# A linear-attention and ELU feed-forward kernel: u of the first four spans in quarters of the array, y's last quarter by DMA from span 2 on, a smaller v, and a new order of the opening

## The chip, the cores and the metric

The kernel runs on one core of one Trainium2 chip. The metric is the device time of one launch in microseconds; 0.2% of it, about what a measurement of this kernel can tell from no change, is 1.0 us.

## The reference, cut to what matters

```python
# q, k, v, alpha: 4 batches x 8 heads x 768 steps x 48
for t in range(S):
    state = alpha[:, :, t, :, None] * state + einsum('bhd,bhe->bhde', k[:, :, t], v[:, :, t])
    y[:, :, t] = einsum('bhd,bhde->bhe', q[:, :, t], state)
x = y.transpose(0, 2, 1, 3).reshape(3072, 384)
h = x @ w_in                                     # 384 -> 2048
g = where(h > 0, h, exp(min(h, 0)) - 1)
out = g @ w_out                                  # 2048 -> 384
```

All inputs and the output are float32.

## The kernel before, in words

**Spans.** A batch's 768 steps are cut into 6 spans of 128 steps, so there are 24 spans, 0 to 23; two neighbouring spans make a block of 256 tokens, 0 to 11. Within a span the recurrence is done by matmuls on two chunks of 64 steps (index c or x), for 4 pairs of heads (n, two heads a = 0, 1 to a pair). For span i the code has small functions, called tokens, that are named by two or three letters: `L`, `LA`, `LB` load q, k and alpha; `LV` loads v; `SC` forms the running product of alpha (`P`) by a scan on DVE; `LN`, `EX` its inverse on ACT; `KA`, `KB`, `KC`, `SQ` scale k and q (DVE or POOL, by the tables `KAV` to `SQV`); `TP`, `KN` (spans 0 to 5, on PE and ACT) or `TA`, `TB` (later, on DVE) transpose k; `S` is the score matmul and `MK` its mask; `U` (L380) is the product of transposed k and v for either chunk; `UA`, `UB`, `UC` (L421 to L443) turn u into the states that the second chunk and the next span start from; `Y` (L489) multiplies scores by v and q by the state. `XH`, `XP`, `XL` split y into an upper and a lower part, fp32r each, in the tile `xt` of the block.

**The form of u.** For spans from `QU` = 6 on, `U` hands over to `U4` (L367), which gives every matmul one quarter of the array (64 rows by 64 columns), so that four of them run side by side; u of chunk 1 is then only that chunk's own sum, and `UB` subtracts it from the state that `UA` has made. For spans 0 to 5 `U` makes two passes by halves: chunk 1 sums over all 128 steps, in 128 rows by 64 columns, and chunk 0 over 64. In span 1 (`UPE`) the old state is added to u on PE, by two matmuls with a matrix `minus` (`UP`, L414), and `UA` is a copy on ACT.

**y's last quarter.** y has 4 pairs of 96 features, but `xt` holds 3 rows of 128: each of these takes one pair's 2 x 48 features and 2 x 16 features of the last pair. For spans below `DIRECT` = 4 the last pair is made first (`YL`), copied to SBUF by ACT (`Y3`), and spread into the three by six matmuls with a selecting matrix `sel` (L497) ahead of the other three pairs. For later spans all four pairs are made at once, ACT and DVE split the last pair into `y3` like the rest, and `XD` (L541) moves it into `xt` by two DMAs of the SP queue.

**Feed-forward.** Block b goes through 8 steps j of 256 hidden features: `A.b.j` (18 matmuls, L655) makes h; `RA`, `RB` (ACT), `RC` (DVE) make the ELU; `GH` (ACT) and `GL` (DVE, L692) split it; `O.b.j` (12 matmuls, L706) adds to the output, which `Z` copies and stores. Weights arrive as raw 64-bit words (`F.f`, 768 KB each, 16 of them); DVE decodes a pair of them (`DA`, `DB`, `DC`, 128x1536 each, 8 pairs), `WH` (ACT) rounds to the upper part, `WL` forms the lower part (POOL, for some DVE, or PE and ACT by `WP`).

**What sets the order.** No scheduler does. The string `START` lists the tokens of the opening (spans 0 to 11, blocks 0 to 3 in part, all the weights), the string `STEADY` a period that is repeated after it. Each token records its instructions when it is called, so the lists fix what stands in which place on every engine's in-order queue and on the SP queue that issues the DMAs. PSUM tiles come from a pool of eight banks.

Of the kernel before, what the change touches and what calls it, by code (L numbers as in the profile page):

```python
# [49 lines left out]
U.1 XH.0 F.6 DC.0 UP.1 LN.2 XP.0 EX.2 KA.2 SQ.2 MK.1 UA.1 F.5 WH.0 WP.0 YL.1 F.1 F.3 UC.1 Y3.1 KB.2 SC.3 KC.2  # L50
WH.2 XL.0 PC.2 LN.3 DA.2 EX.3 SQ.3 Y.1 DB.2 KA.3 XH.1 TP.2 WP.2 DC.2 KB.3 KN.2 DA.1 DB.1 XP.1 KC.3 U.2 XL.1
WL.2 LC.0 WL.0 S.2 A.0.0 RA.0.0 WH.6 WL.6 F.7 A.0.1 MK.2 UB.2 UA.2 TP.3 LV.3 UC.2 S.3 L.4 KN.3 F.9 YL.2 U.3
WH.4 SC.4 WL.4 Y3.2 Y.2 UA.3 PC.3 RB.0.0 MK.3 XH.2 DA.3 SQ.4 DC.1 DB.3 YL.3 LN.4 XL.2 Y3.3 UB.3 A.0.2 LV.4
WH.3 EX.4 F.10 CA.0 F.8 WL.3 Y.3 A.0.3 XH.3 UC.3 DC.3 XL.3 L.5 F.12 RA.0.1 KA.4 KB.4 A.1.1 A.1.0 LV.5 F.11
# [34 lines left out]
def gla_elu_ffn(ctx: ExitStack, tc: tile.TileContext, qka, vv, vn, wgt, out):  # L89
# [174 lines left out]
    @tok  # L264
    def ZS(i):
        if EARLY <= i < QS:
            for a in range(2):
                nc.gpsimd.memset(win[i]["st"][64 - 64 * a:128 - 64 * a, a], 0.0)


    @tok
# [95 lines left out]
    def U4(i):  # L367
        d = win[i]
        q4, begun = shared(i)
        d["u"] = [t[:, 0:NP * D].rearrange("p (n e) -> p n e", n=NP) for t in q4]  # L370
        for n in range(NP):
            for x, a in QUADS if i % NW < NW - 1 else QUADS[::2]:
                r = slice(64 * x, 64 * x + 64)
                nc.tensor.matmul(d["u"][x][64 * a:64 * a + 64, n, :], lhsT=d["kn"][r, n, a, :],  # L374
                                 rhs=d["vn"][r, 2 * n + a, :], start=(n == 0 and x not in begun), stop=True,
                                 skip_group_check=True)
        begun.update((0, 1) if i % NW < NW - 1 else (0,))

    @tok
    def U(i):  # L380
# [4 lines left out]
        d["u"] = [u[:, 0], u[:, 1]]
        m = 64 if i < EARLY else D
        for x in ((1, 0) if i % NW < NW - 1 else (0,)):
            r = slice(0, C) if x == 0 and i < EARLY else slice(0, 128)
            v = d["vn"] if x or i < EARLY else v0[i % 2].rearrange("p (h e) -> p h e", e=D)
            for n in range(NP):  # L390
                for a in range(2):
                    nc.tensor.matmul(d["u"][x][64 * a:64 * a + m, n, :], lhsT=d["kn"][r, n, a, 0:m],  # L392
                                     rhs=v[r, 2 * n + a, :],
                                     start=(x == int(i % NW < NW - 1) and n == 0), stop=True, skip_group_check=True)
# [9 lines left out]

    def diff(i, out, r, x):
        u = win[i]["u"][x][r]
        half = i >= QU and x == 1
        if (i % NW == 0 or i in UPE) and not half:
            nc.scalar.mul(out=out, in_=u, mul=-1.0)  # L409
        else:  # L410
            nc.vector.tensor_tensor(out=out, in0=state(i, r, int(half)), in1=u, op=ALU.subtract)  # L411
# [556 lines left out]
```

## Time and profile before

| | |
|---|---|
| median of 3 runs | 504.48 us (504.24 to 504.65) |
| span of the profiled execution, first to last instruction | 502.5 us |
| time outside that span (median less span) | 2.0 us |
| TensorE clock granted, mean | 0.999 |
| HBM read, written | 53.53 MB, 4.72 MB |

The profile is of one execution. PE is the matmul engine's row, PEld its weight loads, which run beside the matmuls; DVE, ACT and POOL are the vector, scalar and general engines; SPq is the queue of SP that issues nearly all DMAs. A row of a timeline gives the start and the length in us, then engine, line, operation, output tile and inputs. A float32 matmul stands as two records; an fp32r one as one.

### The profile page before, as it was taken

The numbers are of one execution on the slowest core, as the hardware profiler recorded it, in microseconds if no ns is written. First come the engines' busy times: TensorE is split into PE (matmuls) and PEld (weight loads), VectorE is DVE, ScalarE is ACT, GpSimd is POOL, SyncE is SP. The second block draws the span as 40 slices with busy tenths as digits, with TensorE's granted clock in tenths as the row PEclk, the third lists the DMA queues.
The fourth block names the chain that finished last, engine by engine and source line by source line (L and its number), as shares of the span: only waits on it lengthen the run. The fifth ranks groups of instructions, "written<-read, shape, count | busy, mean of one in ns | idle before, by whom it ended". The sixth has DMA issues, their size and how long they took to land.

```text
span 502.5 us, 13254 instructions
## 1 busy us (share of the span) xinstructions
PE 492.4 (98%) x5404; PEld 476.0 (95%) x5404; DVE 386.6 (77%) x807; ACT 289.5 (58%) x689; POOL 129.4 (26%) x111
## 2 busy tenths in 40 slices
...
DMA  8999324222521145226135145234332321110001
GB/s 311 412 411 382 91 95 165 64 59 100 190 59 64 57 130 178 65 83 219 54 119 178 48 119 182 63 112 172 82 112 97 95 76 44 56 42 8 3 33 36
DMA packets 22403, 61.13 MB, mean 122 GB/s; under 512 B 2880, under 2 KB 9792, under 8 KB 22336
## 3 DMA queue, kind: packets, MB, share of 16 engines
...
HBM read 53.53 MB, written 4.72 MB: 116 GB/s over the span
## 4 chain that ended last, share of the span: by engine, by line
PE 96%; DVE 2%; ACT 1%; issue 1%; ACTq 0%
PE o L706 40%; PE h L655 40%; PE y L458 4%; PE y L453 2%; PE q L374 2%; PE q L330 2%; PE u L392 1%; PE sc L346 1%; PE wp L126 1%; PE y L497 1%; PE tp L282 1%; DVE kn L292 0%; PE yl L453 0%; PE wd L628 0%; DVE st L358 0%
## 5 line engine op out<-in xcount | busy, mean ns | idle before, releaser
L655 PE MATMUL h<-xt,w 128*128 128x256 f32 x1728 | 215.0, 282 | 0.0
L655 PEld LDWEIGHTS h<-xt,w 128*128 128x128 f32 x1728 | 209.3, 188 | 1.8
L706 PE MATMUL o<-w,gh 128*128 128x384 f32 x768 | 199.3, 341 | 0.6 <-ACT gh L679 0.6
L706 PEld LDWEIGHTS o<-w,gh 128*128 128x128 f32 x768 | 136.9, 188 | 1.6 <-ACT gh L679 0.8
L706 PE MATMUL o<-w,gl 128*128 128x384 f32 x384 | 130.0, 339 | 0.1
L679 ACT CAST gh<-h 128x512 fp32r<-128x512 f32 x96 | 55.9, 583 | 79.6 <-DVE h L673 39.3
L692 DVE TENSOR_TENSOR gl<-h,gh 128x512 fp32r<-128x512 f32 x96 | 65.5, 687 | 35.5 <-ACT gh L679 34.2
L292 DVE STREAM_TRANSPOSE kn<-qka 32x128 f32<-32x128 f32 x288 | 87.0, 302 | 4.5
L663 ACT ACTIVATE r<-h 128x512 f32<-128x512 f32 x96 | 57.0, 595 | 47.2 <-PE h L655 40.7
L673 DVE SCALAR_TENSOR_TENSOR h<-r,h 128x512 f32<-128x512 f32 x96 | 64.6, 689 | 16.9 <-ACT r L668 16.1
L706 PEld LDWEIGHTS o<-w,gl 128*128 128x128 f32 x384 | 72.1, 188 | 0.4 <-DVE gl L692 0.4
L231 POOL TENSOR_TENSOR qka<-qka,R 128x512 f32<-128x512 f32 x19 | 26.1, 1375 | 164.6 <-DVE gl L692 127.6
L668 ACT ACTIVATE r<-r 128x512 f32<-128x512 f32 x96 | 59.4, 631 | 0.7
L261 POOL TENSOR_TENSOR st<-qka,P 64x512 f32<-64x512 f32 x36 | 42.8, 1189 | 21.7 <-DVE P L209 16.2
L358 DVE TENSOR_TENSOR st<-q,mask 64x256 f32<-64x256 f32 x72 | 30.4, 422 | 12.0 <-ACT vs L409 9.2
L209 DVE TENSOR_TENSOR_SCAN P<-qka,first 128x516 f32<-128x516 f32 x24 | 30.6, 1275 | 1.6 <-DMA qka<-in_qka_dram 1.2
L236 POOL TENSOR_TENSOR R<-P,R 128x512 f32<-128x512 f32 x20 | 24.2, 1211 | 27.3 <-DVE qka L231 25.9
L218 ACT ACTIVATE R<-P 128x512 f32<-128x512 f32 x24 | 15.2, 632 | 27.8 <-DVE P L209 27.8
L411 DVE TENSOR_TENSOR vs<-vs,q 48x192 f32<-48x192 f32 x30 | 10.5, 350 | 19.1 <-PE q L330 16.9
L511 ACT ACTIVATE y<-y 128x128 fp32r<-128x128 f32 x20 | 5.5, 275 | 30.0 <-PE y L458 26.6
L639 POOL TENSOR_TENSOR w<-spare,w 128x768 fp32r<-128x768 f32 x7 | 15.8, 2256 | 26.0 <-ACT w L619 13.9
L611 ACT ACTIVATE ck<-ck,lim 128x384 f32<-128x384 f32 x32 | 20.6, 644 | 0.1
...
## 6 DMA issues: line engine op xcount, KB each, us to landing
...
raw<-in_wgt_dram SPq DMA_DIRECT2D x16, 768.0 KB, 12.3
...
xt<-y SPq DMA_DIRECT2D x40, 48.0 KB, 2.3
...
```

The source lines that it names most:

```text
L209: nc.vector.tensor_tensor_scan(out=P.rearrange("p n w -> p (n w)"), data0=t[:, 2 * NP * W:], data1=first.rearrange("p n w -> p (n w)"), in ...
L231: eng(KAV, i).tensor_tensor(out=d["kt"], in0=d["kt"], in1=d["R"], op=ALU.mult)
L261: eng(SQV, i).tensor_tensor(out=st[r, a], in0=d["q"][r], in1=pw(i)[r], op=ALU.mult)
L292: nc.vector.transpose(out=kn[32 * t:32 * t + 32, :, 32 * g:32 * g + 32], in_=d["kt"][32 * g:32 * g + 32, :, 32 * t:32 * t + 32])
L358: nc.vector.tensor_tensor(out=d["st"][r, a, :, c * C:(c + 1) * C], in0=d["s4"][a][o], in1=mask[o].unsqueeze(1).broadcast_to([64, NP, C]), ...
L655: nc.tensor.matmul(h[:, f, :], lhsT=t[:, wi, ws], rhs=x[:, c, xi, :], start=(f == 0 and k == 0), stop=(k == 8), skip_group_check=True)
L663: nc.scalar.activation(out=r, in_=d["h"], func=AF.Relu, scale=-1.0)
L668: nc.scalar.activation(out=d["r"], in_=d["r"], func=AF.Exp, scale=-1.0)
L673: nc.vector.scalar_tensor_tensor(out=d["h"], in0=d["r"], scalar=-1.0, in1=d["h"], op0=ALU.add, op1=ALU.max)
L679: nc.scalar.copy(out=gh, in_=d["h"])
L692: nc.vector.tensor_tensor(out=gl, in0=d["h"], in1=d["gh"].bitcast(F32), op=ALU.subtract)
L706: nc.tensor.matmul(o[:, 0:DM], lhsT=gt[:, f, ms], rhs=t[:, wi, f * DM:f * DM + DM], start=(j == 0 and f == 0 and k == 0), stop=(j == NJ - ...
```

## The change

Five things are changed at once.

1. `QU` = 6 becomes the set `UQ`: spans 0 to 3 too take `U4`. With it `UPE` is empty: the two matmuls of `UP` in span 1 go; `UA` of span 1 moves from ACT to DVE; `UB` of spans 0 and 1 is now a DVE subtraction (it did not exist there).
2. `DIRECT` = 4 becomes 2: spans 2 and 3 lose `YL`, `Y3` and the `sel` matmuls, make four pairs in one `Y`, and take `XH`, `XL` with `y3` and the two DMAs of `XD`. For spans 0 and 1, y and yl now share a PSUM tile.
3. v of spans from 6 on is loaded without its doubled quarter: two DMAs of 64 x 576 instead of 64 x 768 words each. `U4` finds v in the first or the last part of the tile by the new `vrow`.
4. In `U4` the weights of spans from 6 on are 48 columns wide, not 64, as only 48 of the rows of u are read.
5. `START` is a new list of the same steps; two zeroed tiles `v0` that nothing used go, and the two unused steps `V0` and `ZS`.

```diff
-DIRECT = 4
+DIRECT = 2
-QU, QS = 6, 6
+UQ, QS = (0, 1, 2, 3, *range(EARLY, NWIN),), EARLY
-WPE, XPE, GPE, UPE = (0, 2), (0, 1), (), (1,)
+WPE, XPE, GPE, UPE = (0, 2), (0, 1), (), ()
 START = """
-LA.0 LB.0 SC.0 LN.0 EX.0 LA.1 KA.0 KB.0 LB.1 SC.1 X.2 LV.0 LN.1 X.2 KC.0 F.2 SQ.0 EX.1 F.0 TP.0 KN.0 S.0 U.0
+LA.0 SC.0 LA.1 LN.0 X.2 LB.0 EX.0 SC.1 LB.1 LN.1 F.0 SQ.0 KA.0 KB.0 KC.0 S.0 F.2 EX.1 KA.1 SQ.1 KB.1 MK.0 TP.0 LV.0
...
-            nc.sync.dma_start(out=vs[0:64, 0:2 * HD], in_=vv[i, 0:64])
-            nc.sync.dma_start(out=vs[64:128, HD:3 * HD], in_=vv[i, 64:128])
+            nc.sync.dma_start(out=vs[0:64, 0:HD + HH], in_=vv[i, 0:64, 0:HD + HH])
+            nc.sync.dma_start(out=vs[64:128, 2 * HD - HH:3 * HD], in_=vv[i, 64:128, 0:HD + HH])
+    def vrow(i, x, a, n):
+        r = slice(64 * x, 64 * x + 64)
+        if i < EARLY:
+            return win[i]["vn"][r, 2 * n + a, :]
+        if a == x:
+            o = HD + n * D + x * HH
+            return vs_t[i % NB][r, o:o + D]
+        return lhs(i, x, a)[r, n * D:(n + 1) * D]
...
     def U4(i):
+        m = 64 if i < EARLY else D
-                nc.tensor.matmul(d["u"][x][64 * a:64 * a + 64, n, :], lhsT=d["kn"][r, n, a, :],
-                                 rhs=d["vn"][r, 2 * n + a, :], start=(n == 0 and x not in begun), stop=True,
+                nc.tensor.matmul(d["u"][x][64 * a:64 * a + m, n, :], lhsT=d["kn"][r, n, a, 0:m],
+                                 rhs=vrow(i, x, a, n), start=(n == 0 and x not in begun), stop=True,
                                  skip_group_check=True)
...
     def diff(i, out, r, x):
-        half = i >= QU and x == 1
+        half = i in UQ and x == 1
...
     def UB(i):
-        if i % NW < NW - 1 and (i >= QU or i % NW and i not in UPE):
+        if i % NW < NW - 1 and (i in UQ or i % NW and i not in UPE):
...
     def YL(i):
-        yl = d["yl"] = psa.tile([128, W], F32, name="yl", tag="pa")
+        d["y"] = psa.tile([128, NP, W], F32, name="y", tag="pa")
+        yl = d["yl"] = d["y"][:, NP - 1]
```

What the new list moves is seen in the order of the queues. First the SP queue, whose rows are the first DMAs of the kernel (128x516 is alpha, 128x1024 q and k, 128x1540 all three; `vs` is v, 128x768 for a span below 6; `raw` is a piece of weights). Before:

```order
L179 DMA qka_123<-in_qka_dram 128x516
L183 DMA qka_123<-in_qka_dram 128x1024
L179 DMA qka_124<-in_qka_dram 128x516
L183 DMA qka_124<-in_qka_dram 128x1024
L191 DMA vs_105<-in_vv_dram 128x768
L565 DMA raw_149<-in_wgt_dram 128x1536 x2
L175 DMA qka_125<-in_qka_dram 128x1540
L191 DMA vs_106<-in_vv_dram 128x768
L191 DMA vs_107<-in_vv_dram 128x768
L175 DMA qka_123<-in_qka_dram 128x1540
L565 DMA raw_254<-in_wgt_dram 128x1536 x2
```

The same queue now:

```order
L175 DMA qka_119<-in_qka_dram 128x516
L175 DMA qka_120<-in_qka_dram 128x516
L179 DMA qka_119<-in_qka_dram 128x1024
L179 DMA qka_120<-in_qka_dram 128x1024
L563 DMA raw_139<-in_wgt_dram 128x1536 x2
L187 DMA vs_105<-in_vv_dram 128x768
L187 DMA vs_106<-in_vv_dram 128x768
L171 DMA qka_121<-in_qka_dram 128x1540
L563 DMA raw_263<-in_wgt_dram 128x1536
L171 DMA qka_119<-in_qka_dram 128x1540
L563 DMA raw_263<-in_wgt_dram 128x1536
L187 DMA vs_107<-in_vv_dram 128x768
```

Both alphas go first, both pieces of the first pair of weights go ahead of v of span 0, and v of span 2 goes behind the second pair of weights (`raw_254` before, `raw_263` now).

Second, DVE around the decoding of that second pair. L209 is `SC`, L581, L587, L593 are `DA`, `DB`, `DC`, L258 is `SQ`, L241 `KC`, L231 `KA`, L236 `KB`; the tile numbers 125 and 123 are spans 2 and 3. Before:

```order
L209 SCALAR_TENSOR_TENSOR P<-qka_123,first 128x516
L241 SCALAR_TENSOR_TENSOR qka_125<-R,qka_125 128x512
L581 TENSOR_SCALAR spare_341<-raw_254 128x1536
L258 TENSOR_TENSOR st<-qka_123,P 128x512
L587 SCALAR_TENSOR_TENSOR spare_341<-raw_254,spare_341 128x1536
L231 TENSOR_TENSOR qka_123<-qka_123,R 128x512
L593 SCALAR_TENSOR_TENSOR spare_341<-raw_254,spare_341 128x1536
L236 TENSOR_TENSOR R<-P,R 128x512
```

The same place now, where L210, L242, L259, L232, L237 and L579, L585 are those lines, and 121 and 119 are spans 2 and 3:

```order
L210 SCALAR_TENSOR_TENSOR P<-qka_119,first 128x516
L579 TENSOR_SCALAR spare_352<-raw_263 128x1536
L242 SCALAR_TENSOR_TENSOR qka_121<-R,qka_121 128x512
L585 SCALAR_TENSOR_TENSOR spare_352<-raw_263,spare_352 128x1536
L259 TENSOR_TENSOR st<-qka_121,P 128x512
L232 TENSOR_TENSOR qka_119<-qka_119,R 128x512
L237 TENSOR_TENSOR R<-P,R 128x512
L242 SCALAR_TENSOR_TENSOR qka_119<-R,qka_119 128x512
```

`SQ` of span 2 (`st<-qka_121`), on which the score matmul of span 2 waits, used to stand far ahead of the second pair and stands now behind two of its three decodings.

Third, the SP queue where block 1's last quarter goes to `xt`, now (before, the first rows of this kind, for spans 4 and 5, come behind all of the weights):

```order
L563 DMA raw_626<-in_wgt_dram 128x1536
L543 DMA xt<-y_611 16x6x128 x2
L171 DMA qka_119<-in_qka_dram 128x1540
L543 DMA xt<-y_630 16x6x128 x2
L189 DMA vs_107<-in_vv_dram 64x576
```

Between the two pairs of DMAs of `XD.2` and `XD.3` stands the load of span 6, and `A.1.2`, the first matmul step of block 1, needs both.

More of the change, by code (lines that the diff above doesn't have):

```diff
@@ L50 @@
[L50 to L54, printed above, removed]
@@ new lines @@
+DA.5 WL.10 O.0.2 SC.5 GL.0.3 DB.5 O.0.3 RB.1.1 WH.8 F.12 RB.1.0 RC.1.1 RC.1.0 GH.1.1 RA.1.3 GH.1.0 GL.1.1 F.14 LC.2
+DC.5 LN.5 WL.8 RB.1.3 GL.1.0 A.0.5 EX.5 PC.4 RC.1.3 A.1.4 UA.4 O.1.0 WH.11 RA.0.5 SC.6 LV.7 KA.5 RB.0.5 LN.6 WH.9
+LV.5 KB.5 O.1.1 RC.0.5 WL.11 SQ.6 GH.1.3 GL.1.2 KC.5 WL.9 DA.6 GL.1.3 GH.0.5 DB.6 DC.6 RA.1.4 O.1.2 F.13 EX.6 TP.5
+A.0.4 RB.1.4 RA.0.4 RC.1.4 GL.0.5 F.15 WH.12 SQ.5 KN.5 RB.0.4 RC.0.4 WH.14 WL.12 CA.2 O.1.3 L.7 U.5 WL.14 S.5 UA.5
+MK.5 A.0.6 PC.5 RA.0.6 A.0.7 GH.0.4 RB.0.6 GH.1.4 GL.0.4 Y.4 KA.6 GL.1.4 RC.0.6 XH.4 SC.7 DA.7 LN.7 Y.5 O.0.4 XL.4
@@ new lines @@
+A.1.5 XH.5 DB.7 GH.0.6 L.8 KB.6 ZV.6 RA.0.7 XL.5 DC.7 SQ.7 O.0.5 RA.1.5 WH.15 WL.15 RB.0.7 GL.0.6 EX.7 O.1.4 RB.1.5
+WH.13 RC.0.7 A.1.7 KA.7 WL.13 KC.6 RC.1.5 RA.1.7 A.1.6 GH.0.7 LV.9 KB.7 CB.2 TA.6 TB.6 GL.0.7 O.0.6 RA.1.6 KC.7
+GH.1.5 O.0.7 RB.1.6 XD.4 GL.1.5 RB.1.7 RC.1.7 U.6 TB.7 RC.1.6 UA.6 O.1.5 UB.6 XD.5 GH.1.6 GL.1.6 PC.6 UC.6 GH.1.7
+SC.8 S.6 MK.6 L.9 TA.7 GL.1.7 A.2.1 Z.0 O.1.6 LN.8 A.2.3 S.7 U.7 EX.8 RA.2.3 O.1.7 RB.2.3 Z.1 RA.2.1 RB.2.1 A.2.6
+YL.2 LC.3 KA.8 PC.7 MK.7 KB.8 KC.8 SQ.8 UA.7 RC.2.1 A.2.0 S.8 UB.7 Y.7 RA.2.6 RC.2.3 RA.2.0 UC.7 SC.9 RB.2.6 Y.6
@@ new lines @@
+GH.2.1 MK.8 GH.2.3 GL.2.1 A.2.2 XH.6 TB.8 RC.2.6 RA.2.2 GL.2.3 XH.7 LN.9 A.2.4 LV.8 XL.6 RB.2.2 RB.2.0 TA.8 RC.2.2
+RC.2.0 XD.6 EX.9 GH.2.0 A.2.5 A.2.7 XL.7 U.8 RA.2.7 RA.2.4 GL.2.0 KA.9 RB.2.4 UA.8 CA.3 PC.8 L.10 O.2.0 YL.3 O.2.1
+GH.2.2 XD.7 RC.2.4 SQ.9 UB.8 UC.8 RA.2.5 A.3.2 GL.2.2 O.2.2 O.2.3 L.11 KB.9 RB.2.5 KC.9 GH.2.6 TB.9 RC.2.5 PC.9 TA.9
+RB.2.7 GL.2.6 RA.3.2 GH.2.4 RC.2.7 GL.2.4 U.9 UA.9 RB.3.2 RC.3.2 UB.9 UC.9 SC.10 GH.2.5 GL.2.5 LN.10 A.3.1 EX.10
+SC.11 RA.3.1 O.2.4 A.3.0 S.9 SQ.10 GH.2.7 GL.2.7 KA.10 RB.3.1 RC.3.1 LN.11 KB.10 A.3.4 RA.3.0 MK.9 O.2.5 O.2.6 GH.3.2
@@ L76 @@
+EX.11 KA.11 RA.3.4 RB.3.0 RC.3.0 O.2.7 GH.3.1 KB.11 A.3.3 LV.10 LV.11 GL.3.1 GL.3.2 GH.3.0 GL.3.0 RA.3.3 CB.3 O.3.0
+O.3.1 RB.3.3 L.12 KC.11 KC.10 RC.3.3 TB.11 GH.3.3 GL.3.3 RB.3.4 TA.11 O.3.2 RC.3.4 TB.10 GH.3.4 GL.3.4 Z.2 TA.10
+PC.10 SQ.11 LC.4
 """
@@ L135, in gla_elu_ffn @@
         nc.gpsimd.memset(t[:, 2 * HD:], 0.0)
-    v0 = [work.tile([128, HD], F32, name=f"v0{i}", tag=f"v0{i}", bufs=1) for i in range(2)]
-    for t in v0:
-        nc.gpsimd.memset(t, 0.0)
     def lhs(i, c, a):
@@ L261, in SQ @@
             eng(SQV, i).tensor_tensor(out=st[r, a], in0=d["q"][r], in1=pw(i)[r], op=ALU.mult)
[L264 to L268, printed above, removed]
     @tok
@@ L388, in U @@
             r = slice(0, C) if x == 0 and i < EARLY else slice(0, 128)
-            v = d["vn"] if x or i < EARLY else v0[i % 2].rearrange("p (h e) -> p h e", e=D)
+            v = d["vn"]
             for n in range(NP):
@@ L438, in UC @@
             for r in rows(i + 1):
-                if i >= QU or i % NW and i not in UPE:
+                if i in UQ or i % NW and i not in UPE:
                     nc.vector.tensor_tensor(out=state(i + 1, r, 0), in0=d["u"][1][r], in1=pe[r], op=ALU.mult)
@@ L492, in Y @@
         nn = NC if direct else NP
-        y = d["y"] = psa.tile([128, nn, W], F32, name="y", tag="pa")
+        if not direct:
+            d["y"] = psa.tile([128, NP, W], F32, name="y", tag="pa")
+        y = d["y"]
         if direct:
```

44 lines of the change are left out of this document (16 added, 28 removed).

## The prediction

> **What bounds the kernel now.** I read the page first, then busy time by stage, then the PE timeline of the opening, then DVE beside it.
>
> ```profile
> span 502.5 us, 13254 instructions
> PE 492.4 (98%) x5404; PEld 476.0 (95%) x5404; DVE 386.6 (77%) x807; ACT 289.5 (58%) x689; POOL 129.4 (26%) x111
> DMA  8999324222521145226135145234332321110001
> PE 96%; DVE 2%; ACT 1%; issue 1%; ACTq 0%
> ```
>
> PE is the chain: it stands idle for 10 us in all, and 96% of the chain is matmuls. So what leaves PE's list leaves the time, if nothing else is late at that place. Whether it is must be read by stage (us, then PE, PEld, DVE, ACT, POOL, clock, DMA share):
>
> ```profile
> 20.00:30.00 10.00, 9.55 (x161) 7.74 (x162) 9.46 (x11) 6.24 (x17) 1.03 (x1) 1.00 1.02 412
> 50.00:60.00 10.00, 10.00 (x76) 9.74 (x74) 9.96 (x12) 7.50 (x14) 5.97 (x3) 1.00 0.45 121
> 60.00:70.00 10.00, 10.00 (x116) 9.88 (x116) 9.93 (x15) 7.74 (x15) 6.45 (x4) 1.00 0.18 56
> 200.00:250.00 50.00, 50.00 (x511) 49.43 (x511) 40.41 (x96) 32.04 (x83) 16.92 (x14) 1.00 0.32 102
> ```
>
> The change takes PE work out between 10 and 45 us, and just there two more resources are full: the DMA engines (share 1.02 from 20 to 30 us, and nines in the page's row up to 50 us) and DVE (9.46 to 9.96 of 10). From 200 us on only PE is full. That is the question of this case: PE's saving is sure, but DVE and DMA must come earlier by the same time.
>
> **PE work removed.** These rows are starts and lengths; I count from start to start.
>
> ```profile
> 18.04 0.92 PE L418 MATMUL u<-vs,minus 128*128 128x192 f32 x4
> 18.66 0.47 PE L516 MATMUL y<-xt,minus 128*128 128x384 f32 x1
> ...
> 35.13 0.68 PE L453 MATMUL yl<-st,vs 48*64 48x64 f32 x16
> 35.74 1.27 PE L392 MATMUL u<-vs,kn 128*64 128x48 f32 x32
> 36.94 0.88 PE L497 MATMUL y<-y,sel 128*64 128x128 f32 x12
> 37.75 1.60 PE L453 MATMUL y<-st,vs 48*48 48x64 f32 x48
> 39.15 0.68 PE L453 MATMUL yl<-st,vs 48*64 48x64 f32 x16
> ...
> 83.55 2.08 PE L453 MATMUL y<-st,vs 48*64 48x64 f32 x64
> 85.56 0.62 PE L706 MATMUL o<-w,gh 128*128 128x384 f32 x2
> ...
> 110.01 0.68 PE L374 MATMUL q<-vs,kn 64*64 64x48 f32 x32
> 110.51 0.66 PE L330 MATMUL q<-st,qka 48*64 48x64 f32 x32
> ```
>
> u by halves takes 1.20 us (35.74 to 36.94), by quarters 0.50 (110.01 to 110.51), or about 0.1 more where another form of matmul follows: 0.58 to 0.70 saved, four times in spans 0 to 3, 2.5 us. `UP.1` goes: 0.62 (18.04 to 18.66). The `sel` matmuls of spans 2 and 3 go: 0.81 each (36.94 to 37.75), 1.6. yl and the three pairs cost 0.61 + 1.40 = 2.01 (35.13 to 35.74, 37.75 to 39.15), all four pairs at once 2.01 (83.55 to 85.56): nothing. Together **4.7 us off PE**, all before the first matmul of block 1.
>
> **Weights 48 wide.** In a quarter, 32 records pass in groups of four, eight groups in 0.50 us, 62 ns a group, for 48 moving columns and for 64 alike (L374 and L330 above). So the moving side doesn't set the pace, and the weight load may. Its mean by width (columns last):
>
> ```profile
> L374 PEld LDWEIGHTS q<-vs,kn 64*64 64x64 f32 x528 | 10.1, 134 | 2.3 <-issue 2.0
> L453 PEld LDWEIGHTS y<-st,vs 64*48 64x48 f32 x96 | 4.9, 120 | 0.2 <-issue 0.2
> ```
>
> 14 ns less for 48. If all of it shows, 8 groups x 14 ns x 18 spans (6 to 23) = 2.0 us. The lower end is 0: no row has both sides 48 wide. The nearest, y with 48 wide weights and 64 moving columns (37.75 above), passes 24 groups of two in 1.40 us, 58 ns, where the 64 wide ones (83.55) pass 32 in 2.01, 63 ns; there the moving side may hold it. I take 10 ns: **1.4 us**, at PE's full stages. The Trainium skill, TensorEngine Tiling (Array Packing), Performance Considerations, has a rule against this part: a matmul carries about 60 cycles of overhead, so below some 60 columns a narrower one is no faster. By that rule this term is 0.
>
> **What is added elsewhere.** DVE gets `UB.0`, `UB.1` and `UA.1` and the two subtractions of `y3`.
>
> ```profile
> L411 DVE TENSOR_TENSOR u<-vs,u 128x192 f32<-128x192 f32 x3 | 1.1, 351 | 0.0
> L534 DVE TENSOR_TENSOR y<-y,y 128x128 fp32r<-128x128 f32 x20 | 5.7, 286 | 6.1 <-ACT xt L512 6.1
> xt<-y SPq DMA_DIRECT2D x40, 48.0 KB, 2.3
> ```
>
> 3 x 0.27 + 2 x 0.2 (back to back some 0.08 of each length lies beside its neighbour) = 1.2 us on a full DVE. ACT trades two copies and one negation for two reads of y, and has 2 us free in every ten. The smaller v saves DMA bytes where DMA isn't full (loads of span 6 and later): nothing. Two idle memsets of POOL go: nothing.
>
> **What the new order does to the opening.** Three waits, each by bytes queued or DVE work from rows.
>
> ```profile
> raw<-in_wgt_dram SPq DMA_DIRECT2D x1, 768.0 KB, 9.4
> 3.16 1.00 SPq L565 DMA_DIRECT2D raw<-in_wgt_dram  x2
> 23.22 0.96 DVE L581 TENSOR_SCALAR spare<-raw 128x1536 int32<-128x1536 int32 x1 [0.51 <-DMA raw<-in_wgt_dram]
> L587 DVE SCALAR_TENSOR_TENSOR spare<-raw,spare 128x1536 int32<-128x1536 int32 x4 | 7.0, 1754 | 0.1
> L593 DVE SCALAR_TENSOR_TENSOR spare<-raw,spare 128x1536 int32<-128x1536 int32 x4 | 7.4, 1860 | 0.0
> 29.25 4.54 PE L655 MATMUL h<-xt,w 128*128 128x256 f32 x36
> ```
>
> First, the seventh DMA of before (the second `raw`, issued 3.7) lands at 3.7 + 9.4 = 13.1. Now v of span 0 is seventh, behind the same bytes, so u of span 0 starts at 13.1, not 11.2. That is early and only idles PE. Second, `DA.2` waited for its weights until 23.22; they now have 384 KB less ahead of them, 0.9 us at 412 GB/s: 22.3. Behind it stand `DA` 0.9, `KC` 0.6, `DB` 1.7, `SQ.2` 0.6 until the score matmul of span 2 can start at 26.2, then S 1.0, u 0.6: `A.0.1` at 27.9, against 29.25 for the first A before. PE then needs to `A.1.2`: two A 4.4, `TP`, S, u 2.2, two `Y` 4.0, `TP` 0.5, two A 4.3, u and S of span 4 2.1 = 17.5, so 45.4. Third, that matmul needs `XD.3`. DVE has 18.3 us between `DA.2` and the end of `XL.3` (eleven 128x512 steps at 0.6, 6.7; five of the long decodes `DA`, `DB`, `DC` at 0.9 or 1.7, 6.9; a scan 1.2; two `XL`, a `WL` and five 128x192 steps 3.5), so 23.2 + 18.3 = 41.5, say 42.0; two issues and 2.3 us of landing make 45.7, and the load of span 6 that stands between may hold it 0.7: 46.4. PE waits 1.0 there.
>
> DVE goes on, and beside POOL its steps run over their length:
>
> ```profile
> 43.27 2.25 DVE L593 SCALAR_TENSOR_TENSOR wm<-raw,wm 128x1536 int32<-128x1536 int32 x1
> 47.10 1.95 DVE L209 TENSOR_TENSOR_SCAN P<-qka,first 128x516 f32<-128x516 f32 x1
> 55.88 1.43 DVE L581 TENSOR_SCALAR spare<-raw 128x1536 int32<-128x1536 int32 x1
> 57.23 0.68 DVE L673 SCALAR_TENSOR_TENSOR h<-r,h 128x512 f32<-128x512 f32 x1
> 57.83 1.75 DVE L587 SCALAR_TENSOR_TENSOR spare<-raw,spare 128x1536 int32<-128x1536 int32 x1
> 60.69 3.86 DVE L593 SCALAR_TENSOR_TENSOR spare<-raw,spare 128x1536 int32<-128x1536 int32 x2
> ```
>
> A plain step takes 0.60 (57.23 to 57.83), a long decode 1.7. To `GL.0.3` there are seven decodes, 10.3, eight plain steps, 4.8, a scan 1.2 and three short ones 0.8, so 17.1; the excess of these rows (0.5, 0.6, 0.4, 0.4) adds 1.9, so 61.0. PE reaches `O.0.3` at 46.4 + 4 A (2.15) + 3 O (2.12) = 61.4: level. After `O.0.3`, `A.0.5` and `A.1.4`, `O.1.0` starts at 67.9 with 14 steps of the feed-forward behind it.
>
> ```profile
> 66.44 2.28 PE L655 MATMUL h<-xt,w 128*128 128x256 f32 x18
> 68.55 0.51 PE L706 MATMUL o<-w,gh 128*128 128x384 f32 x2
> 168.54 0.62 PE L706 MATMUL o<-w,gh 128*128 128x384 f32 x2 [0.63 <-ACT gh L679]
> ```
>
> Before, `O.1.0` started at 68.55 with 13 behind it, which is 70.7 for 14. So of 4.7 us **2.8 arrive and 1.9 are lost** to DVE and DMA. After 70 us DVE has slack and PE sets the pace; the one wait left before the end (168.54) lies where the new list puts four A steps ahead, and I count 0.3 of its 0.74 (with the 0.11 behind it) as gone.
>
> Sum: 2.8 + 1.4 + 0.3 = 4.5. The span of 502.5 becomes 498.0; with the 2.0 outside it, which the median of 504.48 also holds, **500.0 us**.
>
> **The rivals.** *All of it arrives* (0.20): my DVE sums are 2 us too long, as they take every step's price from a stage in which POOL and ACT were also busy, and PE stays full from 30 us on. Then 4.7 + 2.0 + 0.7 = 7.4: 497.1. For it speaks that before, with DVE as full, PE did not wait once between 23 and 168 us; against it the 1.2 us that DVE gets on top.
>
> *The narrow weights bring nothing* (0.17), by the groups of two at 58 against 63 ns with the moving side in the way, as the page's rule has it: 500.0 + 1.4 = 501.4.
>
> *The opening eats it* (0.08): DVE is 3 us later at `GL.0.3` or `O.1.0` (a decode that waits for its weights, as at 23.22, or runs over as the rows above). Then nothing arrives of the 2.8, 503.0, or within 1 us of before.
>
> *Slower* (0.06): `XD.3` is caught in the DMA queue. A weight load took 12.3 us in the median from issue to landing, since the queue was that deep:
>
> ```profile
> raw<-in_wgt_dram SPq DMA_DIRECT2D x16, 768.0 KB, 12.3
> ```
>
>  If the DMA queue still holds weights when `XD.3` is issued at 42, it lands at 42 + 12.3 = 54.3, and PE, in order, has nothing else: 7.9 us more than in my forecast, 507.9. It decides from a landing after 46.4 + 4.5 = 50.9. Against it: SP waits for `XL.2` first, so only 770 KB can be ahead, 1.9 us.
>
> That the change does nothing is excluded by the PE order, where the six `sel` matmuls of spans 2 and 3 are no more.
>
> **How the numbers follow.** My forecast has 0.49: 500.0, with 498.6 to 501.4 of its own for the two ends of the weights' term and 1 us of DVE. The range goes from 497.2 (nearly all arrives) to 502.8 (the opening eats it); some 0.1 lies below and 0.1 above. Faster by over 0.2% (1.0 us, below 503.5): the forecast, the first two rivals and a little of the third, 0.88. Within 0.2%: the rest of the third and some of what no case names, 0.06. Slower: the fourth, 0.06.
>
> **What would show it.** Right: u in spans 0 to 3 by quarters with 0.50 to 0.62 us each; no `sel` in spans 2 and 3; groups of four in L374's successor at 52 ns; idle PE at `A.1.2` near 45 us with the DMAs of `xt` as releaser; `O.1.0` near 68 us. Wrong: PE full from 28 us on (then the first rival), groups at 62 ns (the second), a PE wait for `gl` of several us at 60 to 68 us (the third), or a wait for `xt` until after 51 us (the fourth).

## The result, and the profile after

The changed kernel takes 519.65 us (median of 4 runs, 519.47 to 520.47), the kernel before 504.56 us beside it (4 runs): ratio 1.0293, 95% interval 1.0276 to 1.031. It is 15 us slower; 500.0 had been forecast, and the range ended at 502.8.

The page of the changed kernel, its span, its PE, the granted clock and the chain:

```profile
span 517.8 us, 13224 instructions
PE 495.2 (96%) x5376; PEld 478.6 (92%) x5376; DVE 401.0 (77%) x812; ACT 288.3 (56%) x690; POOL 133.4 (26%) x109
PEclk8899799799999999999999999999999999999999
PE 67%; DVE 4%; issue 1%; ACT 0%; DVEq 0%
```

PE was 96% of the chain and is 67%. The clock row (a slice is 12.9 us) has four slices below nine in its first 104 us. Busy time by stage of the changed kernel (us, then PE, PEld, DVE, ACT, POOL, clock, DMA share):

```profile
10.00:20.00 10.00, 9.92 (x207) 8.58 (x205) 8.72 (x12) 3.77 (x10) 1.56 (x1) 0.69 1.02 415
40.00:50.00 10.00, 7.96 (x123) 7.30 (x117) 10.00 (x14) 3.46 (x14) 1.92 (x1) 1.00 0.19 53
50.00:60.00 10.00, 6.52 (x40) 6.55 (x41) 9.97 (x11) 8.38 (x16) 6.77 (x4) 0.66 1.01 365
80.00:90.00 10.00, 8.62 (x67) 7.90 (x66) 9.96 (x9) 4.88 (x10) 5.49 (x4) 1.00 0.44 158
90.00:100.00 10.00, 8.65 (x71) 8.43 (x73) 3.84 (x6) 3.73 (x9) 4.55 (x5) 0.66 0.42 159
200.00:250.00 50.00, 50.00 (x600) 49.22 (x590) 41.28 (x96) 32.62 (x82) 12.19 (x10) 1.00 0.41 132
```

PE is no longer full from 40 to 60 and from 80 to 100 us, and DVE is, up to 90 us. What PE waited for (us in total, times, longest):

```profile
PE h L653 <- DMA xt<-y: 4.1, 1, 4.1
PE sc L340 <- issue: 2.5, 1, 2.5
...
PE q L324 <- DVE gl L690: 1.4, 1, 1.4
PE sc L340 <- DVE st L259: 1.4, 1, 1.4
PE h L653 <- DVE w L637: 1.4, 1, 1.4
PE u L387 <- ACT kn L305: 1.3, 1, 1.3
```

The sum closes. All gaps of PE over 0.03 us make 17.75 us to the end of its last matmul at 513.0, against 5.5 to 497.9 before: 12.26 more. In three stretches of 6.83 us, from 9.4, 50.4 and 91.3 us, PE's clock is halved; it worked 6.5, 3.7 and 6.8 us in them, and half of that, 8.5, is lost. 12.26 + 8.5 - 15.1 (513.0 less 497.9) = 5.7 us of PE work is saved, where 6.1 was forecast. So the saving came, and 20.8 us of waiting and slow clock came with it.

One thing of the changed list is read off its order: it has `UB.2` ahead of `UA.2`. `UB.2` subtracts from what `UA.2` has yet to write, so the state behind span 2 holds its second chunk's sum alone and lacks the first chunk's and what came from the spans before. The same instructions run.

### The profile page after: what moved, and what is told of

Its sections match the earlier page's. It is cut to its first block, busy times and chain, and to the rows that moved or that the text cites. A ratio compares the mean times of both kernels' runs of the same rounds, so it can differ in the third digit from the quotient of the medians.

```text
span 517.8 us, 13224 instructions
## 1 busy us (share of the span) xinstructions
PE 495.2 (96%) x5376; PEld 478.6 (92%) x5376; DVE 401.0 (77%) x812; ACT 288.3 (56%) x690; POOL 133.4 (26%) x109
## 4 chain that ended last, share of the span: by engine, by line
PE 67%; DVE 4%; issue 1%; ACT 0%; DVEq 0%
PE o L704 31%; PE h L653 30%; PE y L453 3%; DVE kn L286 2%; PE q L324 1%; PE q L369 1%; DVE h L671 1%; DVE gl L690 1%; DVE st L352 0%; DVE P L210 0%; ACT r L661 0%; DVE vs L435 0%; DVE q L406 0%; ACT r L666 0%; DVE qka L242 0%
## 5 line engine op out<-in xcount | busy, mean ns | idle before, releaser
L653 PE MATMUL h<-xt,w 128*128 128x256 f32 x1728 | 219.6, 285 | 6.6 <-DMA xt<-y 4.1
L653 PEld LDWEIGHTS h<-xt,w 128*128 128x128 f32 x1728 | 213.6, 192 | 9.4 <-DVE h L671 4.2
L232 POOL TENSOR_TENSOR qka<-qka,R 128x512 f32<-128x512 f32 x19 | 25.0, 1317 | 195.7 <-DVE gl L690 116.5
L262 POOL TENSOR_TENSOR st<-qka,P 64x512 f32<-64x512 f32 x36 | 46.6, 1294 | 23.5 <-DVE P L210 14.1
L210 DVE TENSOR_TENSOR_SCAN P<-qka,first 128x516 f32<-128x516 f32 x24 | 30.0, 1254 | 1.4 <-DMA qka<-in_qka_dram 0.9
L237 POOL TENSOR_TENSOR R<-P,R 128x512 f32<-128x512 f32 x20 | 26.5, 1326 | 14.9 <-DVE qka L232 13.7
L219 ACT ACTIVATE R<-P 128x512 f32<-128x512 f32 x24 | 15.2, 633 | 20.8 <-DVE P L210 20.8
L509 ACT ACTIVATE y<-y 128x128 fp32r<-128x128 f32 x22 | 6.1, 278 | 30.8 <-PE y L453 27.2
L406 DVE TENSOR_TENSOR vs<-vs,q 48x192 f32<-48x192 f32 (+1 forms) x33 | 11.5, 347 | 15.3 <-PE q L324 15.0
L637 POOL TENSOR_TENSOR w<-spare,w 128x768 fp32r<-128x768 f32 x7 | 15.4, 2217 | 14.6 <-ACT w L617 14.5
```

The lines of the kernel that those rows point to most:

```text
L210: nc.vector.tensor_tensor_scan(out=P.rearrange("p n w -> p (n w)"), data0=t[:, 2 * NP * W:], data1=first.rearrange("p n w -> p (n w)"), in ...
L237: eng(KBV, i).tensor_tensor(out=d["R"], in0=pw(i), in1=d["R"], op=ALU.mult)
L653: nc.tensor.matmul(h[:, f, :], lhsT=t[:, wi, ws], rhs=x[:, c, xi, :], start=(f == 0 and k == 0), stop=(k == 8), skip_group_check=True)
```

## The experiments

**Order or content?** My first theory was that the new list costs the time and the content saves it. First the new content in the old list:

```diff
 START (of the kernel before):
-UP.1 ... UB.0 ... UB.1 ... UB.2 UA.2
+UA.0 UB.0 ... UA.1 UB.1 ... UA.2 UB.2 ... XL.2 XD.2 ... XL.3 XD.3
```

> The changed kernel's content in the order of the kernel before; only UB.0, UB.1, XD.2 and XD.3 are put where their inputs are ready, UB.2 stands behind UA.2 (the changed kernel has it ahead of UA.2, so there the state behind span 2 lacks its first chunk), and UP.1 is out. Theory (the order costs the time, the content saves 4.7 + 1.4 us of PE): 499, 497.5 to 500.5, clock 1.0 throughout, no PE wait over 1 us for xt at the first matmul of block 1. Rival (the content itself costs: y's last quarter by DMA and 1.2 us more DVE make xt late in any order): 504 or more, with a PE wait of 3 us or more for xt at block 1.

520.56 us, ratio 1.0296 (1.0253 to 1.0339): the rival's number. But its trace shows a fault of this trial's own, a wait of 9.1 us:

```profile
PE h L652 <- DMA xt<-y: 9.1, 1, 9.1
```

SP stood in `XD.2` until DVE's `XL.2` was done at 47 us, 1.5 MB of weights were issued behind it and went ahead of `XD.3`. Second, the old content in the new list:

```diff
 START (of the changed kernel):
+UP.1 ahead of UA.1; YL.2 Y3.2 behind S.3; YL.3 Y3.3 ahead of TP.4, Y.3 behind it
-XD.2 XD.3
```

> The content of the kernel before in the order of the changed one; the steps that only the old content has (UP.1, YL.2, Y3.2, YL.3, Y3.3) are put ahead of their readers, XD.2 and XD.3 are out. Theory (the order costs it): 515 to 522, with the clock halved around 10 us and a wait of 2 us or more ahead of S.0; block 1 needs no DMA here, so its wait may be smaller than 4.1 us, and 512 is the lowest that the theory bears. Rival (the content costs it): 503 to 506.

521.83 us, 1.0313 (1.0269 to 1.0357): as slow as the changed kernel with none of its content and no DMA ahead of block 1. So the list alone costs as much. The first trial, placed better, and then without y's DMA:

```diff
-UA.0 UB.0 ... XL.2 XD.2 ... XL.3 XD.3
+UB.0 UC.0 ... UB.1 UC.1 ... F.10 ... F.8 ... XL.3 XD.2 XD.3
```

> The content of the changed kernel in the old order once more, the four steps placed with more care: UB.0 and UB.1 right ahead of UC.0 and UC.1 (in the first trial DVE waited in UB.0 for u of span 0 with MK.0 queued behind it), XD.2 and XD.3 both behind XL.3 and behind the weight loads F.10 and F.8 on SP (in the first trial SP waited in XD.2 until 47.0 us, and 1.5 MB of weights went ahead of XD.3). Theory (y's last quarter by DMA is worth its price only where the order leaves PE other work until it lands; the rest of the content saves 5 to 6 us): XD.3 lands near 52.5 us, PE waits some 4 us for it instead of 9.1, in all 509 to 514. Rival (the content costs 15 us in any order): 517 to 522.

```diff
-DIRECT = 2
+DIRECT = 4
```

> The same, but y's last quarter of spans 2 and 3 goes by the `sel` matmuls as in the kernel before (no XD.2, no XD.3): of the change the quarters of u, the smaller v and the narrow weights are left, in the old order. Theory: PE saves 3.1 + 1.4 and no transfer stands ahead of block 1, so 500 to 502.5. Rival (DVE is full from 30 us on, so the 0.8 us that UB.0, UB.1 and UA.1 add and PE's saving only make PE wait for DVE): 503.5 to 505.

516.04 us, 1.0194 (1.0123 to 1.0264), with 5.1 us of wait for `xt`, and 505.02, 0.9982 (0.995 to 1.0014). y's last quarter by DMA costs 11 us in the old list, between the two theories; the rest of the content neither gains nor loses there (the rival was right). Both halves of the change are thus slow by themselves, and adding them up explains nothing.

In the old list the cost can be read off the queues. SP works in order. It stood in `XD.2` for DVE's `XL.2` and issued nothing from 29.4 to 44.6 us, so the load of span 5, which the run without y's DMA issued at 29.8 us, was issued at 49.3. DVE then stood idle 4.7 us for that load and 3.6 us for weights, and PE waited another 4.6 us for `gl`. Without y's DMA, DVE waited for no load between 30 and 70 us. In the new list DVE has no such idle time (it waits for no DMA from 22 to 90 us), so the reason there is another one, and the rest of this section looks for it.

**The clock.** Dummy matmuls in three of the waits:

```diff
+hold(n): n matmuls of 128x512 bf16 into the PSUM tile that the next real matmul starts anew
-X.2 (ahead of S.0)
+X.13 ; hold 17 ahead of A.1.2, 7 ahead of U.5, 6 ahead of S.5
```

> The changed kernel with dummy matmuls put into three of its waits (11 ahead of S.0, 17 ahead of A.1.2, 7 ahead of U.5, 6 ahead of S.5), which write PSUM that the next real matmul starts anew. The waits stay, the clock should not fall. Theory (about 8.5 us of the loss is work at half clock): 509 to 513, clock 1.0, gaps of PE in real work as before them. Rival (the waits alone cost it, and what ran at half clock lay in the shade of other waits): 517 to 521 in spite of a full clock.

517.83 us, 1.0218 (1.0176 to 1.0261); the clock stayed full until 125 us. PE's timeline of block 1 with the dummies, then without:

```profile
49.78 3.83 PE L131 MATMUL h<-first 128*128 128x512 bf16 x17 [0.69 <-DVE vs L443]
53.26 4.62 PE L663 MATMUL h<-xt,w 128*128 128x256 f32 x36
57.72 0.51 PE L714 MATMUL o<-w,gh 128*128 128x384 f32 x2
```

```profile
53.48 6.14 PE L653 MATMUL h<-xt,w 128*128 128x256 f32 x36 [4.12 <-DMA xt<-y]
59.46 0.52 PE L704 MATMUL o<-w,gh 128*128 128x384 f32 x2
```

With the clock full from the start block 1 begins at 53.26 instead of 53.48: what ran at half clock in the opening was not on the path. Then 1.7 us are won (57.72 against 59.46), and at `U.5` nothing is left of them (89.89 against 89.30, though 1.3 of that are the dummies themselves, which had to wait for their PSUM tile). Most of the 8.5 us at half clock lay in the shade of DVE: the rival.

**One wait after the other.** If DVE is the bound, less DVE work helps, and an earlier landing doesn't:

```diff
 START (of the changed kernel):
-DB.1 ... DB.3 ... DB.4
```

> The changed kernel without the second decode pass of weights 1, 3 and 4 (DB.1, DB.3, DB.4: their low words are left out, so the weights are coarser): 3 x 1.7 us of DVE work less ahead of the step S.5 at 91 us. New theory (DVE, not PE, sets the changed kernel's pace from 30 to 91 us): S.5 starts 5 us earlier or more, in all 510 to 515. Rival (the wait for the DMA of y at block 1 and the halved clock cost it): only DB.1 stands ahead of XL.3, so block 1 starts 1.7 us earlier and the time is 516.5 to 518.5.

```diff
-UC.3 XD.2 KN.4 L.6 WH.1 XD.3
+UC.3 XD.2 KN.4 WH.1 XD.3 L.6
```

> The changed kernel with the load of span 6 (L.6, 770 KB) behind XD.3 on SP instead of ahead of it. Both expect XD.3 to land some 2 us earlier, near 51 us, and the wait ahead of A.1.2 to shrink from 4.1 to about 2.2 us. New theory (DVE sets the pace): S.5 stays at 91 us within 0.7, in all 518.5 to 520. Rival (the landing sets it): all of it arrives, with less at half clock, 515 to 517.5.

517.28 us, 1.0228 (1.0155 to 1.03), and 520.21, 1.0283 (1.021 to 1.0355). The second is as the DVE theory has it, 0.2 us above its range: `XD.3` landed at 50.6, block 1 began at 50.9 instead of 53.5, and 3.9 us of waits for `gl` followed. The first is not, and its time is the rival's: 5 us less DVE work moved `S.5` by 1.45 us only, from 91.35 to 89.90. So not the amount of DVE's work. Then the waits themselves were moved out of the way, each on top of the one before:

```diff
 START (of the changed kernel), late:
-... KC.5 WL.9 ... TP.5 A.0.4 ... WH.12 SQ.5 KN.5
+... KC.5 SQ.5 WL.9 ... TP.5 KN.5 A.0.4 ... WH.12
```

> The changed kernel with two steps moved: KN.5 on ACT right behind TP.5's transposes, ahead of WH.12 (which waits for the decode DC.6), and SQ.5 on DVE behind KC.5, ahead of that decode. Theory (the waits of 1.31 us at U.5 and 1.38 us at S.5 are chains that the new order itself makes, and the halved clock behind them costs 3.4 us more; they came out the same with 5 us less DVE work): 512.5 to 515, clock full around 90 us. Rival (DVE as a whole is late there, so the wait shows up at the next step): 517 to 520.

```diff
-XH.2 Y3.3 TP.4 WL.4 DB.1 RC.0.1 XL.2 ... XH.3 ... DA.3 XL.3 DC.1 UC.3 XD.2 KN.4 L.6 WH.1 XD.3 WL.1 DB.3
+XH.2 XH.3 Y3.3 TP.4 WL.4 XL.2 XL.3 RC.0.1 ... UC.3 DB.1 DC.1 XD.2 KN.4 WH.1 XD.3 L.6 WL.1 DA.3 DB.3
```

> The same, and block 1's wait taken out too: XL.2 and XL.3 stand right behind WL.4 on DVE (DB.1 and DA.3, needed later, stand behind them), and the load L.6 behind XD.3 on SP. Theory: XD.3 lands before 49.4 us, A.1.2 doesn't wait, its 4.1 us and 1.9 us at half clock go: 507 to 510.5. Rival (DVE's decodes come next, as the waits of 2.2 us at 64 us did in the run with L.6 behind): block 1 starts in time, but half or more comes back as waits by 85 us: 511 to 514.

```diff
-the list's start
+the list's start up to U.0 as in the kernel before
```

> The same, and the opening of the kernel before up to U.0 (q of span 0 loaded ahead of the decays of span 1, v of span 0 earlier, SC.1 behind KB.0). Theory (the 0.9 us of wait and the 3.3 us at half clock of the opening were only hidden behind block 1's wait): clock full from the start, 2 to 4 us less than the kernel without this step, 504 to 508. Rival (the opening is off the path, since DVE's queue sets when PE can go on at 20 to 43 us): within 1 us of the kernel without this step.

517.3 us, 1.0227 (1.0203 to 1.0251); 517.98, 1.0267 (1.024 to 1.0294); 516.86, 1.0228 (1.0209 to 1.0247). The waits at `U.5`, `S.5` and block 1 went, and the time stayed. In the third the opening's wait of 4.0 us was only split into two, 2.4 and 1.7, with 6.8 us at half clock behind them, so that trial did not do what it was to test. What PE waited for in the second and the third:

```profile
PE h L652 <- DVE gl L689: 5.5, 4, 2.8
PE sc L339 <- DVE qka L241: 4.0, 1, 4.0
```

```profile
PE h L652 <- DVE gl L689: 5.6, 4, 2.8
PE tp L275 <- issue: 2.4, 1, 2.4
```

The waits of h for `gl`, 0.6 us in the changed kernel, had grown to 5.5, which neither theory had; the second is slower than either allowed. DVE was late whatever stood in its list.

**Why DVE is late.** I then read DVE's steps beside POOL's instead of by themselves. In the changed kernel, 34 to 43 us:

```profile
34.60 1.29 POOL L232 TENSOR_TENSOR qka<-qka,R 128x512 f32<-128x512 f32 x1 [9.70 <-ACT R L224]
34.67 2.83 DVE L591 SCALAR_TENSOR_TENSOR spare<-raw,spare 128x1536 int32<-128x1536 int32 x1
35.97 2.58 POOL L237 TENSOR_TENSOR R<-P,R 128x512 f32<-128x512 f32 x1
38.52 1.18 POOL L259 TENSOR_TENSOR st<-qka,P 128x512 f32<-128x512 f32 x1
38.59 1.66 DVE L242 SCALAR_TENSOR_TENSOR qka<-R,qka 128x512 f32<-128x512 f32 x1 [0.22 <-POOL R L237]
39.70 2.21 POOL L637 TENSOR_TENSOR w<-spare,w 128x768 fp32r<-128x768 f32 x1
40.17 2.57 DVE L637 TENSOR_TENSOR w<-spare,w 128x768 fp32r<-128x768 f32 x1
42.79 0.38 PE L653 MATMUL h<-xt,w 128*128 128x256 f32 x1 [1.37 <-DVE w L637]
```

Whichever of the two engines comes second stands still until the other's step is over. `DC.2` (34.67) starts 0.07 us after POOL's `KA.4`, whose end is 35.89, and ends 1.6 us after that, at 37.5. `KB.4` came behind it and takes 2.58 instead of 1.2, to 38.55. `KC.4` (38.59) waits for `SQ.4`'s end at 39.70, then takes its 0.6; `WL.4` (40.17) waits for POOL's weights, that had waited for `KC.4`. DVE loses 1.1 + 1.0 + 1.6 us in 8 us. Steps that take an input from PSUM (`RC`, `GL`, `MK`, u) run beside POOL at their full speed: of the 192 `RC` and `GL` of this trace 48 began beside a POOL step, and none took over 0.70 us. This is what the Trainium skill says (SBUF — State Buffer, Who interferes with whom): DVE and GpSimd share a pair of ports, a DVE step with two inputs in SBUF contends with a GpSimd step that reads SBUF, and the first holds it for its whole length. The trace agrees for the steps with two inputs.

I took each DVE step's time until 90 us (up to the next step's start where that is earlier) less the lower quartile of all steps of its shape, and summed: about 4.6 us before, 14.1 us in the changed kernel, 14.1 in the one with the late and the block's waits moved. To test that these stops are the cause, POOL's `WL` was made a step that writes but doesn't read (the weights' low parts are left out), in the changed kernel, in the one before, and in the one with the waits moved; and four POOL steps were given to DVE:

```diff
-eng(WLV, f).tensor_tensor(out=wgts[f][:, 1], in0=wm[p][:, k], in1=wgts[f][:, 0].bitcast(F32), op=ALU.subtract)
+nc.gpsimd.memset(wgts[f][:, 1].bitcast(F32), 0.0)       # on POOL only
```

> The changed kernel in which GpSimd's low parts of the weights (the subtraction WL, all but 0, 2 and 4) are a memset to zero: GpSimd writes the same tile, but reads nothing (the weights' low parts are left out). All the rest, DVE's list too, is the same. Theory (a step of DVE that starts while GpSimd runs a step with inputs in SBUF stands still until that ends; 8.8 us of DVE's stretched time before 95 us lie beside WL, and the new order put them there): S.5 starts 4 us earlier or more, 508 to 514. Rival (it is the amount and place of DVE's own work in the new order): 517 to 520.

> The same edit in the kernel before. Theory: its DVE is stretched by 3 us beside WL until 95 us, and PE there waits for nothing, so 503.5 to 505.3. Rival (the memset also saves work that every order has on its path): 500 to 503.

> The kernel with KN.5, SQ.5, XL.2, XL.3 and L.6 moved, with the same memset in WL's place. Theory: with those waits moved and the stretching beside WL gone, DVE keeps up, 504 to 510. Rival: 514 to 518, as without the memset.

```diff
-KAV, KBV, SQV = (0, 1, 2, 3, 10), (0, 3, 5, 6), (1, 2, 3, 5)
+KAV, KBV, SQV = (0, 1, 2, 3, 4, 10), (0, 2, 3, 4, 5, 6), (1, 2, 3, 4, 5)
```

> The changed kernel, full computation, with KB.2, KA.4, KB.4 and SQ.4 on DVE instead of GpSimd: DVE gets 4 x 0.6 = 2.4 us of work, and the 3.9 us go for which DA.2, DC.2, KC.4 and the step behind them were stretched beside these. Theory: DVE is 1 to 2 us earlier at XL.3, 516.5 to 519. Rival (DVE's own work is the bound): 2 us more, 520.5 to 523.

511.79 us, 1.0109 (1.0069 to 1.0148): 7.9 less. 504.79, 0.999 (0.9971 to 1.0009): nothing. 507.75, 1.0027 (1.0004 to 1.005): 10.2 less than with the subtraction. 517.62, 1.0232 (1.0192 to 1.0272): 2.0 less than the changed kernel, in spite of 2.4 us more for DVE. The sums of lost time are 6.9, 2.3, 6.4 and 9.8 us. As a memset is also shorter, it was made as long:

```diff
+for _ in range(3):
     nc.gpsimd.memset(wgts[f][:, 1].bitcast(F32), 0.0)
```

> The changed kernel with the memset in WL's place three times over (3 x 0.74 = 2.2 us, as long as the subtraction was), so that GpSimd is busy as long and the weights' low parts (zero here) are ready no earlier by its own time. Theory (what counts is that GpSimd's step reads SBUF): 510 to 514, as with one memset. Rival (it helped that the low parts were ready 1.4 us earlier, or that GpSimd was free): 515 to 519.

510.91 us, 1.0111 (1.0069 to 1.0152). POOL's groups, changed kernel and this one (x39 is three to each `WL`), and DVE's `DC` in both:

```profile
L637 POOL TENSOR_TENSOR w<-spare,w 128x768 fp32r<-128x768 f32 x7 | 15.4, 2217 | 14.6 <-ACT w L617 14.5
...
L591 DVE SCALAR_TENSOR_TENSOR spare<-raw,spare 128x1536 int32<-128x1536 int32 x4 | 9.4, 2360 | 0.0
L591 DVE SCALAR_TENSOR_TENSOR wm<-raw,wm 128x1536 int32<-128x1536 int32 x4 | 8.4, 2089 | 0.0
```

```profile
L642 POOL MEMSET w<- 128x768 f32 x39 | 30.8, 795 | 16.6 <-DVE spare L591 9.1 <-issue 3.0 <-DVE wm L591 2.9
...
L591 DVE SCALAR_TENSOR_TENSOR spare<-raw,spare 128x1536 int32<-128x1536 int32 x4 | 8.1, 2018 | 0.0
L591 DVE SCALAR_TENSOR_TENSOR wm<-raw,wm 128x1536 int32<-128x1536 int32 x4 | 7.0, 1748 | 0.0
```

POOL is as busy, 30.8 us for these 13 against 15.4 for 7 of them, and the decodes are short again. For the steps with two inputs it is the reading. (`DA`, with one input, stops beside the memset too: one ran 1.60 us instead of 0.95.) In this run PE still waits 4.2 us for `xt` at block 1, which begins at 52.0 us, 1.5 earlier; the other 7 us come from the stretch to 98 us, where `U.5` and `S.5` no longer wait and the clock is halved for 3.4 us instead of 13.7.

**The same in one step.** The old list with the new content but y's DMA had a wait of 1.71 us that the kernel before has not. All engines there, 32 to 35 us:

```profile
32.48 1.81 POOL L636 TENSOR_TENSOR w<-spare,w 128x768 fp32r<-128x768 f32 x1 [11.09 <-ACT w L616]
32.49 2.33 DVE L241 SCALAR_TENSOR_TENSOR qka<-R,qka 128x512 f32<-128x512 f32 x1
...
34.89 0.65 PE L275 MATMUL tp<-ident,qka 128*128 128x128 f32 x4 [1.71 <-DVE qka L241]
```

`KC.3` starts some 20 ns after POOL's `WL.0` and takes 2.33 us instead of 0.68; in the kernel before it started first:

```profile
31.91 0.68 DVE L241 SCALAR_TENSOR_TENSOR qka<-R,qka 128x512 f32<-128x512 f32 x1
...
33.08 1.83 POOL L639 TENSOR_TENSOR w<-spare,w 128x768 fp32r<-128x768 f32 x1 [12.05 <-DMA qka<-in_qka_dram]
```

Moved, with DVE and PE of that run below:

```diff
-KN.2 DA.1 DB.1 XP.1 KC.3 U.2
+KN.2 KC.3 DA.1 DB.1 XP.1 U.2
```

> The old order with u by quarters, the smaller v and the narrow weights, y without DMA, and one step moved: KC.3 on DVE ahead of DA.1 instead of behind DB.1. Where it stood it started 19 ns after GpSimd's WL.0 and stood still for 1.66 us, and PE waited 1.7 us for it at span 3's transposes. Theory: most of these 1.7 us arrive, ratio 0.993 to 0.997. Rival (DVE is late there anyway, the next step waits): 0.9975 to 1.0.

```profile
30.25 0.69 DVE L241 SCALAR_TENSOR_TENSOR qka<-R,qka 128x512 f32<-128x512 f32 x1
...
36.09 0.60 PE L275 MATMUL tp<-ident,qka 128*128 128x128 f32 x4
```

504.28 us, 0.997 (0.995 to 0.999): the wait is gone and the kernel is faster than before, at the upper edge of what was expected. That the time is better than without the move (0.9982, 0.995 to 1.0014) is not shown, as the intervals overlap, and the rival's range lies partly within this one.

**The narrow weights, and a better kernel.** The narrow weights alone on the kernel before, and with the smaller v and u of spans 2 and 3 by quarters, which gives DVE nothing new:

```diff
-d["u"][x][64 * a:64 * a + 64, n, :], lhsT=d["kn"][r, n, a, :]
+d["u"][x][64 * a:64 * a + D, n, :], lhsT=d["kn"][r, n, a, 0:D]
```

> The kernel before with u's weights 48 wide from span 6 on and nothing else. Theory (13 ns for each group of four, 8 groups, 18 spans, as the changed kernel's trace has it): 502.7, 502.3 to 503.2. Rival (a matmul has a floor of about 60 columns, so nothing is gained): 504.3 to 504.8.

```diff
-UQ, QS = (0, 1, 2, 3, *range(EARLY, NWIN),), EARLY
+UQ, QS = (2, 3, *range(EARLY, NWIN),), EARLY     # DIRECT = 4, UPE = (1,), old list
```

> The order of the kernel before with a part of the change that gives DVE no new work: u by quarters in spans 2 and 3 only, the narrow weights, the smaller v; UP.1 and the `sel` matmuls stay. Theory (what is left at full PE stages arrives: 0.7 of the narrow weights, as their own run's trace ended, and 0.6 of span 3's u): ratio 0.997 to 0.998. Rival (PE's saving in the opening all becomes waiting for DVE, and of the narrow weights nothing can be measured): 0.999 to 1.001.

504.25 us, 0.9992 (0.9966 to 1.0018), not to be told from no change; and 503.26, 0.9972 (0.9947 to 0.9997), faster than both kernels.

## Why the prediction was wrong, step by step

**PE's saving** was right in kind: 5.7 us against 6.1. u's quads have become shorter, from 0.50 us to 0.39 for the first of a pair. In the changed kernel:

```profile
314.61 0.57 PE L369 MATMUL q<-vs,kn 64*48 64x48 f32 x32
315.00 0.66 PE L324 MATMUL q<-st,qka 48*64 48x64 f32 x32
```

That is 49 ns for a group of four instead of 62 and, over 15 full spans at 0.10 and three half ones at 0.07, 1.7 us; 1.4 had been put in. The rule of some 60 columns, by which the term was 0 (Trainium skill, TensorEngine Tiling (Array Packing), Performance Considerations), does not hold for these rows, if it is read as a rule on the weights' width; the section speaks of the free dimension and does not say of which operand, and here the moving side stayed at 48 columns. In the time, though, little of it is seen: the last matmul of the run with this edit alone ended at 497.4 against 497.9. PE was busy for 1.1 us less there and waited 0.5 us more; where the rest of the 1.7 goes is open.

**The step that failed** is DVE's time in the opening. I had "DVE has 18.3 us between `DA.2` and the end of `XL.3`", each step at its shortest length, and `XL.3`'s end at 42.0. In the trace of the changed kernel:

```profile
22.09 0.69 DVE L232 TENSOR_TENSOR qka<-qka,R 128x512 f32<-128x512 f32 x1 [0.92 <-ACT R L224]
...
22.86 2.04 POOL L237 TENSOR_TENSOR R<-P,R 128x512 f32<-128x512 f32 x1 [10.99 <-DVE qka L232]
23.84 1.88 DVE L579 TENSOR_SCALAR spare<-raw 128x1536 int32<-128x1536 int32 x1
...
47.52 0.55 DVE L536 TENSOR_TENSOR xt<-y,xt 128x384 fp32r<-128x384 f32 x1
```

`DA.2` began at 23.84, not 22.3, as DVE had waited 0.92 us for ACT ahead of `KA.2` and had that step and the scan of span 3 still to do, where the forecast had put only the landing of the weights; it took 1.88 us instead of 0.95, as POOL's `KB.2` ran until 24.9; and `XL.3` ended at 48.07. These 6.1 us are 1.5 of late start, 0.9 of stop at `DA.2`, and the 1.1 + 1.0 + 1.6 shown above. I had the rows: "beside POOL its steps run over their length", and I added 1.9 us of excess, but only for the stretch after `XL.3`, and at the size that the old list had. I took for a mean what depends on which of two steps starts first, and that is just what a new list changes.

**The fourth rival** (0.06) named the right place, a wait for `xt` at block 1, but not the reason: no weights stood ahead of `XD.3` (the DMA share was 0.01 from 40 to 45 us), only the load of span 6, `L.6`, that the forecast had priced at 0.7 us. The queue around it:

```profile
45.73 1.39 SPq L543 DMA_DIRECT2D xt<-y  x2
47.23 0.53 SPq L171 DMA_DIRECT2D qka<-in_qka_dram  x1
48.13 1.24 SPq L543 DMA_DIRECT2D xt<-y  x2
```

`XD.3` landed at 53.2 us, 5.1 us after its issue and not 12.3; the rival decided from 50.9. But the load in front cost only some 2 us of it (50.6 with the load behind); the rest was DVE, late at `XL.3`. Its 507.9 us was too little for another reason: the loss ended there, as in all my cases. I had written that "after 70 us DVE has slack and PE sets the pace". DVE was full until 90 us, `O.1.0` began at 76.5 and not at 67.9, and `U.5`, `S.5` and the half clock behind them took another 6.1 us (1.31 + 1.38 + 3.4). The four waits from 125 us on (1.42, 0.49, 1.06 and 0.63, 3.6 in all), the `q` of 1.4 in the table among them, stayed within 0.2 us in every run with the new list and the new content; nothing was tried on them. The sum had the opposite there: of the 0.74 us that PE waited at this place before, it counted 0.3 as gone. The first two are not stops beside POOL, which ran nothing from 117.0 to 129.2 and from 134.1 to 151.6 us; that the order of DVE's own list makes them is likely, but not shown.

**Of the signs named,** "PE full from 28 us on" and "a PE wait for `gl` of several us at 60 to 68 us" did not show: PE waited for `xt` until 53.5 us, the sign put down for the fourth.

What is left over of the loss is not settled in full. With the waits moved and POOL's `WL` not reading, 507.75 us is still slower than before, by 1.4 us by the ratio and 2.5 by the medians. Its trace has 4.05 us of wait and two windows of half clock in the opening, which that run kept, and 3.6 us in the four late waits, 2.8 more than the kernel before has there.
